# FFT filter with two feed-forward layers on one core: the second layer's weights become float32 beside the single blocks and wait in DRAM, and the sums of weights move behind a group's first products

## The chip, the cores and the metric

One core of a Trainium2 chip runs the whole program. The metric is the device time of one execution in microseconds (us); the median of three runs of the kernel before is 1181.71 us (1181.01 to 1183.72).

## The reference

```python
X = np.fft.rfft(x, axis=1)                  # x: 2 x 3008 x 256
y = np.fft.irfft(X * (filt_r + 1j * filt_i), n=3008, axis=1)   # 6016 tokens of 256
h = y @ w_in                                # 256 x 2048, float64
g = np.where(h >= 1, h, np.where(h <= -1, 0, (h + 1) ** 2 / 4))
x = g @ w_out                               # 2048 x 256
h = x @ w_in2
out = (h / (1 + np.exp(-h))) @ w_out2
```

The weights of both layers arrive as float64, 8 bytes a number.

## The kernel before, in words

**Layers.** Tokens lie along the free dimension, in 12 blocks of 500 or 502. Every product is made of float32 parts that TensorE can multiply (a high part, rounded, and a low part, the remainder): three matmuls, high by high, high by low, low by high. A layer's 2048 hidden features are 16 slices of 128; a slice `f` has a weight tile of 128x512 (its part of `w_in` in the first 256 columns, of `w_out` in the last 256).

**Weights.** For slice `f` of layer `m`, `fetch_weight` (L146) loads 128x512 int64 words by two DMAs on SyncE's queue (SP), `read_weight` (L164) has ScalarE (ACT) make two passes over the words (L167, L168), and `form_weight` (L171) has VectorE (DVE) make three (L175 to L177) and GpSimd (POOL) one addition (L178). The result is a float32 tile `wa`, of which three can live at a time. For the first layer, `split_weight` makes high and low parts of it at once.

**Single blocks.** The first six blocks of the first layer go one block and one slice at a time: 96 slots of `up` (six matmuls, then ACT's `u` and square and DVE's `g`), `split_g` (ACT's `gh` L362, DVE's `gl` L364) and, five slots later, `down` (six matmuls, L376 to L378). Beside the later slots, up to number 84, runs the rest of the Fourier transform of the second half of x (ACT, DVE and POOL make its high and low parts).

**Groups.** All other work is 72 groups (`group`, L596): nine pairs of blocks (three of the first layer, called wide here, then six of the second), eight groups `j` to a pair, one for each two slices. A group makes 2x2 products by Strassen's seven: its order of PE (TensorE) work is `prod` A11, A12 (bank d, L610), S2, S3, S1, S4, A22, each of three matmuls (L526 to L528), and four `between` steps, 0 to 3, each with the twelve-part `down2` of the group before split into six matmuls. ACT copies the bank `b` after A11, S2 and S1 (`s1`, `u2`, `u4`, L535), since the next product is added on top of it; DVE makes the sums c11, c22, c21 (L612, L647, L664). Each of a group's four results has a `Chain`: in a wide group ACT's `first` (L554) and `square` (L558), DVE's `last` (L563), ACT's `high` (L571) and DVE's `low` (L574); in the second layer one Silu (L550) in place of the first three. The chain "21" of a group is finished in the next one, between its first products.

**Sums of weights.** For Strassen's products each group needs sums of its weights. `sum_first` (L436, first layer) adds high and low part on DVE (L440) and makes four sums (L423 to L426); `round_first` has ACT round them, `rest_first` has POOL subtract (L433). `sum_weight`, `round_weight` and `rest_weight` (L461 to L473) do it for the second layer from its `wa` tiles: four sums on DVE, three roundings on ACT (L430), three remainders on POOL (L433), and the `wa` tiles are then free.

**Who orders it.** The order on every engine is the order of the code. `at(t, fn, ...)` puts a function into an agenda and `due(t)` calls it: t counts slots from NB on, then, from GA = NB + 96, the `between` steps, four to a group, so that GA + 4 q + i is step i of group q. Y = GA + 96 is the first group of the second layer. An engine takes its instructions in that order and waits at the first one that isn't ready; a DMA queue does so too.

In the kernel before, the agenda fetches the second layer's weights from step Y - 38 on and converts them at Y - 34 to Y + 18 (L756 to L761), so from the sixteenth wide group on. The sums for the second layer stand at Y - 26, -18, -10, -3, 3, 9, 15, 21, the first layer's at step 2 of the group two ahead of theirs (L737).

Of the kernel before, what the change touches and what calls it, by code (L numbers as in the profile page):

```python
# [9 lines left out]
F32 = mybir.dt.float32  # L10
# [4 lines left out]
I64 = mybir.dt.int64  # L15
# [18 lines left out]
NFC = DFF // 128  # L34
# [58 lines left out]
def tile_fft_conv_moe_moe(  # L93
# [10 lines left out]
):  # L104
    nc = tc.nc
    ctx.enter_context(tc.manual_schedule())
    HEAD, LAG = 17, 5
    SP, P0, P1, P2, P3, NBX, SZ = 27, 5, 3, 2, 2, 8, 7
    WARM = 6
    CR, CF, CS, CP, RATE, TAIL = 3, 4, 7, 12, 16, 3  # L110
# [3 lines left out]
    dram = ctx.enter_context(tc.tile_pool(name="dram", bufs=1, space=bass.MemoryType.DRAM))  # L114
    W0 = 6
    wp0 = ctx.enter_context(tc.tile_pool(name="wp0", bufs=W0))
    rawp = ctx.enter_context(tc.tile_pool(name="rawp", bufs=2))
# [8 lines left out]

    x2d = dram.tile([2, 128, NTOK], F32, name="x2d")

    nc.scalar.dma_start(fwd1, dft[:96, :128])
    fwd2 = dft_sb[:, 0:128]  # L130
    inv2 = dft_sb[:, 128:256]
# [4 lines left out]
    weights, cv = {}, {}  # L136

    raws = [0]

    def raw_tile(shape, dtype, name, one=False):  # L140

        raws[0] = 0 if one else raws[0] + 1
        tag, bufs = ("raw", 1) if one or raws[0] % 3 == 1 else ("raw2", 2)
        return rawp.tile(shape, dtype, tag=tag, name=name, bufs=bufs)

    def fetch_weight(m, f):  # L146
        w_in, w_out = ((w_in1, w_out1), (w_in2, w_out2))[m]
        raw = raw_tile([128, 512], I64, f"raw{m}_{f}", m == 1 and f < 8)
        nc.sync.dma_start(
            raw[:, :256].rearrange("p (k j) -> p k j", k=2),  # L150
            w_in[:, f * 128:(f + 1) * 128].rearrange("(k p) j -> p k j", p=128),
        )
        nc.sync.dma_start(raw[:, 256:], w_out[f * 128:(f + 1) * 128, :])
        cv[m, f] = raw
# [16 lines left out]
    def form_weight(m, f):  # L171
        raw, a = cv[m, f]
        e = rawp.tile([128, 512], I32, tag="we", name=f"we{m}_{f}", bufs=1)
        ai = a.bitcast(I32)
        nc.vector.tensor_scalar(e, words(raw, I32, 1), -0x80000000, None, ALU.bitwise_and)  # L175
        nc.vector.tensor_scalar(a, a, EXP_MIN, EXP_MAX, ALU.max, ALU.min)
        nc.vector.scalar_tensor_tensor(ai, ai, 3, e, ALU.logical_shift_left, ALU.bitwise_or)  # L177
        nc.gpsimd.tensor_tensor(ai, ai, words(raw, I32, 0), ALU.add)  # L178
        cv[m, f] = a

    def split_weight(m, f, pool):
        a = cv.pop((m, f))
# [227 lines left out]
    NP = NFC // 2  # L410
# [185 lines left out]
    def group(p, j, prev, between):  # L596


        m = PL[p][0]
        wide = m == 0  # L600
# [16 lines left out]
            if not pwide:  # L617
                prev["21"].high()
        k11 = Chain(c11, p, j, "11")
        k11.first()  # L620
        if prev and not pwide:
            prev["21"].low()
        between[0]()
# [4 lines left out]
        u2 = snap(b, p, j, "u2")  # L628
        if pwide:
            prev["21"].square()  # L630
        k11.square()
        if pwide:
            prev["21"].last()
# [49 lines left out]
    NB = NCH + NBX  # L683
# [3 lines left out]
    def at(t, fn, *args):  # L687
        agenda.setdefault(t, []).append((fn, args))
# [32 lines left out]
    for i in range(HEAD, n):  # L721
        t = B1 + SP * (i - HEAD) // 10
# [10 lines left out]
    GA = NB + W1S  # L733
    Y = GA + 4 * NP * (len(PAIRS) - NS // 2)
    for j in range(NP):
        at(GA - 6 + 4 * j, sum_first, j)
        at(GA - 5 + 4 * j, round_first, j)  # L737
        at(GA - 4 + 4 * j, rest_first, j)
    zw = []

    def store(j):
# [11 lines left out]
        s = small_store(f"1_{j}") if j < 6 else [v[:, :384] for v in full[j]]  # L753
        return a, b, s

    for j, t in enumerate((-26, -18, -10, -3, 3, 9, 15, 21)):  # L756
        for i in range(2):
            f = 2 * j + i
            at(Y + t - (9 if j > 3 else 12) + (2 if j > 3 else 4) * i, fetch_weight, 1, f)
            at(Y + t - (6 if j > 3 else 8) + (2 if j > 3 else 4) * i, read_weight, 1, f)  # L760
            at(Y + t - (5 if j > 3 else 7) + (2 if j > 3 else 4) * i, form_weight, 1, f)  # L761
        at(Y + t, sum_weight, j)
        at(Y + t + 1, round_weight, j, store)
        at(Y + t + 2, rest_weight, j)

    def make_ring():
        xr = zp.tile([128, 8, 2, 512], F32R, tag="z0", name="xr")
# [144 lines left out]
```

## Time and profile before

| what | value |
|---|---|
| median of three runs | 1181.71 us |
| the profiled execution: its own time, its span | 1183.22 us, 1181.4 us |
| PE busy | 1133.7 us, 96% of the span, 4931 matmuls |
| ACT, DVE, POOL busy | 817.8, 776.1, 252.1 us |
| mean granted TensorE clock | 0.993 |
| DMA | 55.29 MB, 47 GB/s over the span |

PE is the engine that is busy throughout. Matmuls overlap in the profile, each shown with about 0.39 us while one starts every 0.23 us, so a busy PE may still start fewer matmuls than it could; the starts of the same product in successive groups show the pace better. A wait that belongs to PE or its weight load (PEld) is time lost; a wait of another engine is lost only where PE waits behind it. The clock is 2.4 GHz where it is granted as 1.0, and 1.2 GHz at 0.5.

### The profile page before, as it was taken

Reading aid. Unit: us, or ns where it says so; the run is one execution under the profiler, and the core shown is the slowest. Engines: PE = TensorE matmul, PEld = TensorE weight load, DVE = VectorE, ACT = ScalarE, POOL = GpSimd, SP = SyncE. Lnnn points to the kernel's source line nnn. Section 1 sums busy time; section 2 is a strip of 40 time slices with the busy share of each in tenths; the row PEclk is TensorE's granted clock in tenths of the full one; section 3 lists DMA queues with packets and bytes.
Section 4 is the critical chain, followed back from the end, with each engine's and each line's share of the span. In section 5 each row is a group of like instructions: output and inputs, shape, how many; then the busy total and the mean of one; then the engine's idle time right before and its main releaser. Section 6 shows DMA issues by size and latency. Waiting matters only on the chain. (4 is left out here: it accounts for less than half of the span.)

```text
span 1181.4 us, 14064 instructions
## 1 busy us (share of the span) xinstructions
PE 1133.7 (96%) x4931; PEld 901.7 (76%) x4931; DVE 776.1 (66%) x1226; ACT 817.8 (69%) x1515; POOL 252.1 (21%) x220
## 2 busy tenths in 40 slices
PE   8899999999999999999888889999999999999998
PEld 3477787878888867877666567888888888888887
DVE  6977546666657787677888878545545555555443
ACT  3588767767757777788777776766666666666664
POOL 4677534546401110000132333100000000000000
PEclk9999999999999999999999999999999999999999
DMA  9733022222000000100311140020010200200000
GB/s 241 196 97 101 1 82 61 78 56 82 15 18 1 18 1 1 54 1 1 108 51 36 56 157 1 1 70 1 26 45 1 71 1 1 70 1 1 36 1 36
DMA packets 30983, 55.29 MB, mean 47 GB/s; under 512 B 3552, under 2 KB 18112, under 8 KB 30912
## 3 DMA queue, kind: packets, MB, share of 16 engines
q1 hardware_dynamic: 27200, 47.98, 13.7%
q10 hardware_dynamic: 3712, 6.40, 1.5%
q8 instruction: 39, 0.64, 0.2%
q14 instruction: 32, 0.26, 0.1%
HBM read 42.05 MB, written 12.32 MB: 46 GB/s over the span
## 5 line engine op out<-in xcount | busy, mean ns | idle before, releaser
L377 PE MATMUL o<-gl,wh 128*128 128x502 f32 (+1 forms) x624 | 246.1, 394 | 6.3 <-DVE gl L574 6.2
L376 PE MATMUL o<-gh,wh 128*128 128x502 f32 (+1 forms) x624 | 245.9, 394 | 0.4 <-ACT ob L384 0.3
L378 PE MATMUL o<-gh,wl 128*128 128x502 f32 (+1 forms) x624 | 245.2, 393 | 0.0
L574 DVE TENSOR_TENSOR gl<-c,gh 128x502 fp32r<-128x502 f32 (+1 forms) x288 | 203.4, 720 | 55.2 <-ACT gh L571 53.4
L571 ACT ACTIVATE gh<-c 128x502 fp32r<-128x502 f32 (+1 forms) x288 | 170.5, 618 | 18.1 <-DVE c L563 15.3
L377 PEld LDWEIGHTS o<-gl,wh 128*128 128x128 f32 x624 | 118.4, 190 | 34.4 <-DVE gl L574 10.5
L535 ACT ACTIVATE u<-b 128x502 f32<-128x502 f32 (+1 forms) x144 | 83.1, 577 | 82.6 <-PE b L528 82.6
L376 PEld LDWEIGHTS o<-gh,wh 128*128 128x128 f32 x624 | 118.5, 190 | 27.0 <-ACT ob L384 1.0
L378 PEld LDWEIGHTS o<-gh,wl 128*128 128x128 f32 x624 | 118.5, 190 | 24.6
L364 DVE TENSOR_TENSOR gl<-g,gh 128x502 fp32r<-128x502 f32 (+1 forms) x80 | 63.7, 796 | 76.5 <-ACT gh L362 76.5
L647 DVE TENSOR_TENSOR c<-c,u 128x502 f32<-128x502 f32 (+1 forms) x72 | 48.8, 678 | 94.3 <-ACT u L535 94.3
L550 ACT ACTIVATE c<-c 128x502 f32<-128x502 f32 (+1 forms) x144 | 88.7, 616 | 26.6 <-DVE c L647 25.4
L178 POOL TENSOR_TENSOR wa<-wa,raw 128x512 int32<-128x512 int32 x32 | 47.7, 1492 | 249.9 <-DVE wa L177 166.8
L362 ACT ACTIVATE gh<-g 128x502 fp32r<-128x502 f32 (+1 forms) x96 | 59.9, 623 | 58.6 <-PE o L378 42.0
L664 DVE TENSOR_TENSOR c<-c,u 128x502 f32<-128x502 f32 (+1 forms) x72 | 48.9, 679 | 61.6 <-PE c L528 61.5
L535 ACT ACTIVATE s<-b 128x502 f32<-128x502 f32 (+1 forms) x72 | 42.2, 587 | 59.4 <-PE b L528 58.5
L343 PE MATMUL h<-xh,wh 128*128 128x502 f32 (+1 forms) x192 | 76.5, 399 | 3.8 <-DVE g L356 3.8
L356 DVE SCALAR_TENSOR_TENSOR g<-u,h 128x502 f32<-128x502 f32 (+1 forms) x96 | 64.3, 670 | 23.7 <-ACT u L355 23.7
L345 PE MATMUL h<-xh,wl 128*128 128x502 f32 (+1 forms) x192 | 75.1, 391 | 1.3 <-POOL wl L187 1.3
L344 PE MATMUL h<-xl,wh 128*128 128x502 f32 (+1 forms) x192 | 74.8, 389 | 0.0
L349 ACT ACTIVATE u<-h 128x502 f32<-128x502 f32 (+1 forms) x96 | 55.5, 578 | 21.2 <-PE h L345 20.6
L612 DVE TENSOR_TENSOR c<-d,s 128x502 f32<-128x502 f32 (+1 forms) x72 | 48.9, 680 | 31.4 <-PE d L528 21.1
(197 smaller groups left out, 2409.8 us busy)
## 6 DMA issues: line engine op xcount, KB each, us to landing
f<-in_filt_dram SPq DMA_DIRECT2D x64, 192.0 KB, 4.9
raw<-in_moe_w_in_dram SPq DMA_DIRECT2D x32, 256.0 KB, 2.7
raw<-in_moe_w_out_dram SPq DMA_DIRECT2D x32, 256.0 KB, 3.0
xs<-x2d SPq DMA_DIRECT2D x8, 502.0 KB, 5.3
Z<-in_x_dram SPq DMA_DIRECT2D x16, 192.0 KB, 6.1
x<-in_x_dram SPq DMA_DIRECT2D x16, 192.0 KB, 3.1
xs<-x2d SPq DMA_DIRECT2D x4, 500.0 KB, 4.2
x2d<-ob ACTq DMA_DIRECT2D x4, 251.0 KB, 2.1
```

Of the source, the lines that this page charges most:

```text
L343: nc.tensor.matmul(h, wh[:, s], xh[:, k, :t], start=(k == 0), stop=False)
L344: nc.tensor.matmul(h, wh[:, s], xl[:, k, :t], start=False, stop=False)
L345: nc.tensor.matmul(h, wl[:, s], xh[:, k, :t], start=False, stop=(k == 1))
L356: nc.vector.scalar_tensor_tensor(g, u, 1.0, h, ALU.min, ALU.max)
L364: engine.tensor_tensor(gl, g, gh.bitcast(F32), ALU.subtract)
L376: nc.tensor.matmul(o[e], wh[:, s], gh, start=first, stop=False)
L377: nc.tensor.matmul(o[e], wh[:, s], gl, start=False, stop=False)
L378: nc.tensor.matmul(o[e], wl[:, s], gh, start=False, stop=last)
L535: nc.scalar.activation(v, src, AF.Copy)
L550: nc.scalar.activation(self.g, self.h, AF.Silu)
L571: nc.scalar.activation(self.gh, self.g, AF.Copy)
L574: nc.vector.tensor_tensor(self.gl, self.g, self.gh.bitcast(F32), ALU.subtract)
```

## The change

The conversions of the second layer move from the wide groups to the single blocks: twelve are fetched at every fourth slot from 34 to 78, four more at every second from 83 to 89, and each is converted three slots later. Each result is stored two slots after that into a DRAM tile (`put_weight`, one DMA of 256 KB on SP) and read back (`get_weight`, one DMA on SP, into one of the three `wa` buffers) for `sum_weight`, which now stands at step 0 of a group, with its roundings at step 1 and its remainders at step 2: Y - 24, -20, -16, -8, -4, 0, 4, 8. `sum_first` moves from step 2 two groups ahead to step 0 of the group just ahead of the one that uses it. In a wide group, the chain 11's first ACT instruction moves behind the copy `u2` and the square of the chain 21.

```diff
--- before.py
+++ after.py
@@ -104,7 +104,7 @@
 ):
     nc = tc.nc
     ctx.enter_context(tc.manual_schedule())
-    HEAD, LAG = 17, 5
+    HEAD, LAG, EARLY = 17, 5, 12
     SP, P0, P1, P2, P3, NBX, SZ = 27, 5, 3, 2, 2, 8, 7
     WARM = 6
     CR, CF, CS, CP, RATE, TAIL = 3, 4, 7, 12, 16, 3
@@ -126,6 +126,8 @@
 
     x2d = dram.tile([2, 128, NTOK], F32, name="x2d")
 
+    w2d = [dram.tile([128, 512], F32, name=f"w2d{f}") for f in range(NFC)]
+
     nc.scalar.dma_start(fwd1, dft[:96, :128])
     fwd2 = dft_sb[:, 0:128]
     inv2 = dft_sb[:, 128:256]
@@ -137,15 +139,17 @@
 
     raws = [0]
 
-    def raw_tile(shape, dtype, name, one=False):
-
-        raws[0] = 0 if one else raws[0] + 1
-        tag, bufs = ("raw", 1) if one or raws[0] % 3 == 1 else ("raw2", 2)
+    def raw_tile(shape, dtype, name):
+        raws[0] += 1
+        tag, bufs = ("raw", 1) if raws[0] % 3 == 1 else ("raw2", 2)
         return rawp.tile(shape, dtype, tag=tag, name=name, bufs=bufs)
 
     def fetch_weight(m, f):
         w_in, w_out = ((w_in1, w_out1), (w_in2, w_out2))[m]
-        raw = raw_tile([128, 512], I64, f"raw{m}_{f}", m == 1 and f < 8)
+        if m == 1 and f < EARLY:
+            raw = dp.tile([128, 512], I64, tag="raw", name=f"raw{m}_{f}", bufs=1)
+        else:
+            raw = raw_tile([128, 512], I64, f"raw{m}_{f}")
         nc.sync.dma_start(
             raw[:, :256].rearrange("p (k j) -> p k j", k=2),
             w_in[:, f * 128:(f + 1) * 128].rearrange("(k p) j -> p k j", p=128),
@@ -177,6 +181,13 @@
         nc.vector.scalar_tensor_tensor(ai, ai, 3, e, ALU.logical_shift_left, ALU.bitwise_or)
         nc.gpsimd.tensor_tensor(ai, ai, words(raw, I32, 0), ALU.add)
         cv[m, f] = a
+
+    def put_weight(f):
+        nc.sync.dma_start(w2d[f], cv.pop((1, f)))
+
+    def get_weight(f):
+        cv[1, f] = rawp.tile([128, 512], F32, tag="wa", name=f"wb{f}", bufs=3)
+        nc.sync.dma_start(cv[1, f], w2d[f])
 
     def split_weight(m, f, pool):
         a = cv.pop((m, f))
@@ -617,7 +628,8 @@
             if not pwide:
                 prev["21"].high()
         k11 = Chain(c11, p, j, "11")
-        k11.first()
+        if not wide:
+            k11.first()
         if prev and not pwide:
             prev["21"].low()
         between[0]()
@@ -628,6 +640,8 @@
         u2 = snap(b, p, j, "u2")
         if pwide:
             prev["21"].square()
+        if wide:
+            k11.first()
         k11.square()
         if pwide:
             prev["21"].last()
@@ -733,9 +747,9 @@
     GA = NB + W1S
     Y = GA + 4 * NP * (len(PAIRS) - NS // 2)
     for j in range(NP):
-        at(GA - 6 + 4 * j, sum_first, j)
-        at(GA - 5 + 4 * j, round_first, j)
-        at(GA - 4 + 4 * j, rest_first, j)
+        at(GA - 4 + 4 * j, sum_first, j)
+        at(GA - 3 + 4 * j, round_first, j)
+        at(GA - 2 + 4 * j, rest_first, j)
     zw = []
 
     def store(j):
@@ -753,15 +767,19 @@
         s = small_store(f"1_{j}") if j < 6 else [v[:, :384] for v in full[j]]
         return a, b, s
 
-    for j, t in enumerate((-26, -18, -10, -3, 3, 9, 15, 21)):
+    for f in range(NFC):
+        t = NB + (34 + 4 * f if f < EARLY else 83 + 2 * (f - EARLY))
+        at(t, fetch_weight, 1, f)
+        at(t + 3, read_weight, 1, f)
+        at(t + 3, form_weight, 1, f)
+        at(t + 5, put_weight, f)
+    for j in range(NP):
+        t = Y - 24 + 4 * j + (4 if j > 2 else 0)
         for i in range(2):
-            f = 2 * j + i
-            at(Y + t - (9 if j > 3 else 12) + (2 if j > 3 else 4) * i, fetch_weight, 1, f)
-            at(Y + t - (6 if j > 3 else 8) + (2 if j > 3 else 4) * i, read_weight, 1, f)
-            at(Y + t - (5 if j > 3 else 7) + (2 if j > 3 else 4) * i, form_weight, 1, f)
-        at(Y + t, sum_weight, j)
-        at(Y + t + 1, round_weight, j, store)
-        at(Y + t + 2, rest_weight, j)
+            at(t - 2 + i, get_weight, 2 * j + i)
+        at(t, sum_weight, j)
+        at(t + 1, round_weight, j, store)
+        at(t + 2, rest_weight, j)
 
     def make_ring():
         xr = zp.tile([128, 8, 2, 512], F32R, tag="z0", name="xr")
```

PE's order does not change. On ACT, in a slot of the single blocks (`u2_9` is the ninth slice of block 2, `hl` a part of the Fourier transform), before:

```order
L349 ACTIVATE u2_9_1735<-h2_9_1727 128x502
L362 ACTIVATE gh2_8_1737<-g2_8_1686 128x502
L355 ACTIVATE u2_9_1735<-u2_9_1735 128x502
L234 ACTIVATE hl18_1757<-t1_18_1725 128x384
L234 ACTIVATE hl19_1764<-x19_1651 96x512
L349 ACTIVATE u2_10_1777<-h2_10_1769 128x502
```

and in the change, whose lines are numbered 11 to 14 higher:

```order
L360 ACTIVATE u2_9_1766<-h2_9_1758 128x502
L373 ACTIVATE gh2_8_1768<-g2_8_1717 128x502
L366 ACTIVATE u2_9_1766<-u2_9_1766 128x502
L245 ACTIVATE hl18_1788<-t1_18_1756 128x384
L245 ACTIVATE hl19_1795<-x19_1678 96x512
L171 ACTIVATE wa1_1_1800<-raw1_1_1680 128x512
L172 ACTIVATE raw1_1_1680<-raw1_1_1680 128x512
L360 ACTIVATE u2_10_1816<-h2_10_1808 128x502
```

Two ACT instructions of a conversion now stand ahead of the next slot's `u`.

On ACT, in the fourth group of the third wide pair (names are chain, pair and group: `v112_3` is chain 11 of pair 2, group 3), before:

```order
L554 ACTIVATE v212_2_5688<-c212_2_5652 128x500
L554 ACTIVATE v112_3_5690<-c112_3_5685 128x500
L517 ACTIVATE xr_3228<-xs3_0_5438 128x502
L535 ACTIVATE u22_3_5702<-b2_3_5668 128x500
L558 ACTIVATE v212_2_5688<-v212_2_5688 128x500
L558 ACTIVATE v112_3_5690<-v112_3_5690 128x500
L571 ACTIVATE gh21_2_2_5708<-c212_2_5652 128x500
L535 ACTIVATE u42_3_5725<-b2_3_5668 128x500
L571 ACTIVATE gh11_2_3_5727<-c112_3_5685 128x500
L167 ACTIVATE wa1_4_5745<-raw1_4_5637 128x512
L168 ACTIVATE raw1_4_5637<-raw1_4_5637 128x512
```

and in the change:

```order
L565 ACTIVATE v212_2_5857<-c212_2_5824 128x500
L528 ACTIVATE xr_3387<-xs3_0_5621 128x502
L546 ACTIVATE u22_3_5874<-b2_3_5837 128x500
L569 ACTIVATE v212_2_5857<-v212_2_5857 128x500
L565 ACTIVATE v112_3_5877<-c112_3_5854 128x500
L569 ACTIVATE v112_3_5877<-v112_3_5877 128x500
L582 ACTIVATE gh21_2_2_5882<-c212_2_5824 128x500
L441 ACTIVATE wz_5779<-wb2_5810 128x512
L441 ACTIVATE wz_5779<-wb3_5835 128x512
L441 ACTIVATE sh1_1_5891<-ws1_1_5865 128x384
L546 ACTIVATE u42_3_5904<-b2_3_5837 128x500
```

The conversion is gone, `u2` (`u22_3`) comes ahead of `v112_3`, and three roundings of weights now stand ahead of the copy `u4` (`u42_3`).

On DVE, the sums for the first layer's sixth pair of slices (`wr5`, `ws0_5`), before, between the sums c22 and c21 of group 3:

```order
L647 TENSOR_TENSOR c220_3_4032<-c0_3_4019,u40_3_4026 128x502
L574 TENSOR_TENSOR gl11_0_3_4029<-c110_3_3984,gh11_0_3_4028 128x502
L440 TENSOR_TENSOR wr5_4041<-wh0_10_1009,wl0_10_1010 128x256
L440 TENSOR_TENSOR wr5_4041<-wh0_11_1068,wl0_11_1069 128x256
L423 TENSOR_TENSOR ws0_5_4044<-wr5_4041 128x128
...
L426 TENSOR_TENSOR ws0_5_4044<-wr5_4041,ws0_5_4044 128x128
L664 TENSOR_TENSOR c210_3_4063<-c0_3_4019,u20_3_4003 128x502
```

and in the change, in group 4:

```order
L623 TENSOR_TENSOR c110_4_4292<-d0_4_4288,s10_4_4279 128x502
L585 TENSOR_TENSOR gl12_0_3_4286<-c120_3_4265,gh12_0_3_4285 128x502
L451 TENSOR_TENSOR wr5_4303<-wh0_10_1025,wl0_10_1026 128x256
L451 TENSOR_TENSOR wr5_4303<-wh0_11_1084,wl0_11_1085 128x256
L434 TENSOR_TENSOR ws0_5_4306<-wr5_4303 128x128
...
L437 TENSOR_TENSOR ws0_5_4306<-wr5_4303,ws0_5_4306 128x128
L523 TENSOR_TENSOR xs1_0_4020<-xs1_0_4020 128x502
L574 SCALAR_TENSOR_TENSOR c210_3_4263<-v210_3_4295,c210_3_4263 128x502
```

The sums now stand behind c11 and ahead of the last step of the chain 21 (`c210_3`).

## Rows read from the trace of the kernel before

**Rows 1.** Busy time of the engines in stretches of the span: the single blocks beside the Fourier transform, the last nine wide groups, the next five groups (the second layer's first), and the 42 groups after them. Columns: from and to, length, busy us and count of PE, PEld, DVE, ACT, POOL, granted clock, DMA share, GB/s.
```profile
215.00:345.00 130.00, 127.92 (x618) 107.27 (x617) 85.12 (x126) 89.96 (x170) 56.65 (x53) 1.00 0.19 56
...
548.17:667.40 119.23, 103.34 (x406) 75.64 (x405) 98.11 (x160) 94.57 (x178) 28.44 (x19) 0.97 0.19 62
667.40:732.45 65.05, 55.98 (x226) 42.44 (x225) 51.35 (x79) 45.98 (x86) 26.08 (x19) 0.97 0.22 72
732.45:1162.52 430.07, 430.07 (x1891) 356.36 (x1890) 229.44 (x359) 280.09 (x507) 3.96 (x3) 1.00 0.06 22
```

**Rows 2.** Timeline of PE: the first matmul into bank d of groups 1, 7, 8, 9, 10, 15, 24, 29 and 71 (counted from 0). Columns: start, us, then the instruction.
```profile
383.76 0.39 PE L526 MATMUL d<-xr,wh 128*128 128x502 f32 x1
...
457.51 0.39 PE L526 MATMUL d<-xr,wh 128*128 128x502 f32 x1
...
469.63 0.39 PE L526 MATMUL d<-xr,wh 128*128 128x502 f32 x1
...
479.94 0.39 PE L526 MATMUL d<-xr,wh 128*128 128x502 f32 x1
...
495.74 0.39 PE L526 MATMUL d<-xr,wh 128*128 128x502 f32 x1
...
548.17 0.39 PE L526 MATMUL d<-xr,wh 128*128 128x502 f32 x1
...
667.40 0.38 PE L526 MATMUL d<-xr,wz 128*128 128x502 f32 x1
...
732.45 0.39 PE L526 MATMUL d<-xr,wh 128*128 128x502 f32 x1
...
1162.52 0.39 PE L526 MATMUL d<-xr,wh 128*128 128x500 f32 x1
```

**Rows 3.** Waits between 548.17 and 732.45 us: engine and line, what it waited for, us in total, times, longest.
```profile
PE b L526 <- ACT u L535: 15.1, 15, 1.8
...
ACT wa L167 <- POOL wl L433: 9.0, 4, 2.4
...
PE o L377 <- DVE gl L574: 5.4, 6, 1.5
```

**Rows 4.** Groups of instructions in the same stretch: line, engine, operation, count, busy us in total, mean ns of one, idle time before them and its releasers.
```profile
L178 POOL TENSOR_TENSOR wa<-wa,raw 128x512 int32<-128x512 int32 x16 | 23.2, 1448 | 228.1 <-DVE wa L177 164.7 <-ACT v L554 12.4 <-ACT sh L430 10.8
...
L433 POOL TENSOR_TENSOR wl<-wa,wh 128x512 fp32r<-128x512 f32 x8 | 13.3, 1678 | 0.0
L177 DVE SCALAR_TENSOR_TENSOR wa<-wa,we 128x512 int32<-128x512 int32 x16 | 11.1, 693 | 0.5
L167 ACT ACTIVATE wa<-raw 128x512 f32<-128x512 f32 x16 | 10.6, 662 | 10.1 <-POOL wl L433 9.0 <-ACT ob_9p L384 0.5 <-ACT ob_10p L384 0.5
...
L433 POOL TENSOR_TENSOR sl<-ws,sh 128x384 fp32r<-128x384 f32 x6 | 7.4, 1231 | 0.0
L175 DVE TENSOR_SCALAR we<-raw 128x512 int32<-128x512 int32 x16 | 6.9, 429 | 0.0
...
L430 ACT ACTIVATE wh<-wa 128x512 fp32r<-128x512 f32 x8 | 4.6, 618 | 0.0
```

**Rows 5.** Timeline of a wide group without conversions and without sums of weights: the last matmul of S2, ACT's and DVE's steps up to `u4` (L535 at 543.66), and the first matmul of S4.
```profile
540.39 0.39 PE L528 MATMUL b<-xr,s 128*128 128x502 f32 x1
540.59 0.67 DVE L574 TENSOR_TENSOR gl<-c,gh 128x502 fp32r<-128x502 f32 x1
...
541.29 0.57 ACT L535 ACTIVATE u<-b 128x502 f32<-128x502 f32 x1
...
542.41 1.27 DVE L563 SCALAR_TENSOR_TENSOR c<-v,c 128x502 f32<-128x502 f32 x2 [0.56 <-ACT v L558]
...
543.12 0.63 ACT L571 ACTIVATE gh<-c 128x502 fp32r<-128x502 f32 x1 [0.23 <-DVE c L563]
...
543.66 0.57 ACT L535 ACTIVATE u<-b 128x502 f32<-128x502 f32 x1
...
544.71 0.39 PE L526 MATMUL b<-xr,s 128*128 128x502 f32 x1
```

**Rows 6.** Timeline of a wide group with a conversion at step 1, ahead of `u4`.
```profile
633.35 0.65 ACT L167 ACTIVATE wa<-raw 128x512 f32<-128x512 f32 x1
...
634.45 0.57 ACT L535 ACTIVATE u<-b 128x500 f32<-128x500 f32 x1
...
635.07 0.49 PE L526 MATMUL b<-xr,sh 128*128 128x500 f32 x1 [1.15 <-ACT u L535]
```

**Rows 7.** Timeline of a wide group in which DVE and POOL both read from SBUF.
```profile
587.99 1.30 POOL L178 TENSOR_TENSOR wa<-wa,raw 128x512 int32<-128x512 int32 x1 [9.48 <-DVE wa L177]
588.13 1.69 DVE L574 TENSOR_TENSOR gl<-c,gh 128x500 fp32r<-128x500 f32 x1 [0.28 <-ACT gh L571]
...
589.88 0.49 PE L377 MATMUL o<-gl,wh 128*128 128x500 f32 x1 [1.06 <-DVE gl L574]
```

**Rows 8.** Waits in the single blocks, between 215 and 345 us.
```profile
DVE gl L364 <- ACT gh L362: 42.7, 33, 4.2
```

**Rows 9.** Groups of instructions of `sum_first` between 371.33 and 469.63 us, columns as in rows 4.
```profile
L440 DVE TENSOR_TENSOR wr<-wh,wl 128x256 f32<-128x256 f32 x12 | 4.5, 418 | 0.0
...
L423 DVE TENSOR_TENSOR ws<-wr 128x128 f32<-128x128 f32 x7 | 2.0, 293 | 0.7
```

**Rows 10.** DMA issues of the whole span: line, engine, count, KB each, median us from issue to landing.
```profile
raw<-in_moe_w_out_dram SPq DMA_DIRECT2D x32, 256.0 KB, 3.0
```

## The prediction, made before the change was run

> **What bounds the kernel now.** I read the table of stretches first, then the starts of one product group by group, then the waits of the stretch that loses time, then single timelines there. From 732.45 us to the end PE is busy all the time, and its granted clock is 1.00 [rows 1]: 42 groups take 1162.52 - 732.45 = 430.07 us [rows 2], 10.24 us each. That is PE's own pace and the yardstick for what follows; nothing after 732 us can get faster.
>
> Between 548.17 and 667.40 us nine wide groups take 119.23 us [rows 1, 2]. At 10.24 us they would take 92.2, so 27.0 us are lost. In the next five groups 65.05 - 51.2 = 13.9 us are lost. All sixteen conversions of the second layer lie in these two stretches [rows 4]. That wide groups don't need the extra time by themselves is seen in the five before them: from 495.74 to 548.17 us, without conversions and without sums of weights, they take 52.43 us [rows 2], 10.49 each. Part of the loss is the clock: 0.97 in both stretches [rows 1], so PE had about 3% of 184 us at half work, some 5 us; the rest of the span between has 1.00. The waits name who is late: PE for ACT's copies 15.1 us, PE for DVE's `gl` 5.4, and ACT's conversions for POOL's remainders 9.0, since only three `wa` tiles live [rows 3]. So the wide groups are bound by ACT and DVE, whose order has no room for more work, and the prize is at most 27.0 + 13.9 = 41 us.
>
> **What the conversions cost where they go.** One is 0.66 us twice on ACT, 0.43 twice (the second pass is of the same kind) and 0.69 on DVE, 1.45 on POOL [rows 4]. That is 1.3, 1.55 and 1.45 us, once in four slots. Between 215 and 345 us PE is busy 127.92 of 130 us, ACT only 89.96, DVE 85.12, POOL 56.65 [rows 1]. Even if all twelve of the early conversions fell into these 130 us, ACT would come to 106, DVE to 104 and POOL to 74: none reaches 130. DVE waits there 42.7 us for ACT's `gh` [rows 8], which in turn waits for PE's old `down`: these engines follow PE with a distance fixed by buffers, and a late one catches up. I charge **2 us** for the single blocks; the bounds are 0 (all of it in idle time) and 16 x 0.4 = 6 (each delays PE by a third of what rows 6 show). The four late ones stand where the transform has ended. The new DMAs are 32 of 256 KB; one of that size lands 3.0 us after issue [rows 10], and a stored tile has from the single blocks to the wide groups after 548 us. On SP a storing DMA waits for POOL's addition, and loads of the transform queue behind it; they are issued at least two slots before use, so I cost this at nothing; without that cover it is part of the 6 us.
>
> **What is left in the nine wide groups.** The change leaves five sets of second-layer sums there (steps Y - 24, -20, -16, -8, -4), each with four DVE sums, three roundings ahead of `u4`, and three remainders on POOL. A clean group shows the room [rows 5]: S2 ends at 540.39 + 0.39 = 540.78, `u2` starts only at 541.29, behind `first` of chain 11; `gh` of chain 21 starts at 543.12, `u4` at 543.66, and S4, which needs `u4`, at 544.71. ACT starts an instruction every 0.5 to 0.55 us. In the change `u2` can start at 540.8, and then square, `first`, square and `gh` follow, the last at about 542.9. But DVE has the four sums (4 x 0.3 = 1.2 us, [rows 9]) behind `gl`, which ends near 541.2, so chain 21's `last` runs from 542.5 to 543.1 and `gh` from 543.15. Three roundings of 0.52 us come next, so `u4` ends near 545.9 and S4 waits 1.2 us. The nearest row agrees: a conversion's two instructions at the same place took 1.10 us and PE waited 1.15 [rows 6]. Five times 1.2 is 6.0. In two of the five groups a sum of x (0.67 us, like any two-operand DVE step of that size) stands in the same step, 1.3 more. The first and the last of the nine make four parts of x, as group 7 did, which took 469.63 - 457.51 = 12.12 us [rows 2], 1.9 above pace; 3.0 for both with the earlier `u2`. POOL's remainders beside DVE I put at 0.3 a set, 1.5, and the remaining groups at 0.7. The sum is 12.5, so **14.5 us are gained** (27.0 - 12.5). The bounds are 21 (sets at no more than 0.2) and 7 (2.5 a set and one clock drop of 1.7).
>
> **The five groups after them.** Second-layer groups have one ACT step where wide ones have three, and 42 of them ran at PE's pace [rows 2]; a rounding between `u2` and `u4` fits there. What stopped them was ACT standing at a conversion for POOL's remainder [rows 3]; that wait moves to SP, whose DMA into the third `wa` buffer waits for the remainder instead. I leave 1.5 us for the first, which finishes wide chains, and 0.5 for the others: **11.9 us gained**, bounds 13.5 and 9.
>
> **The first layer's sums.** Their DVE work, 2 x 0.42 + 4 x 0.29 = 2.0 us [rows 9], was between c22 and c21; now it stands ahead of chain 21's `last`, and two roundings ahead of `u4`. By the timeline of rows 5 `last` then starts near 543.3 in place of 542.4, `gh` ends at 544.5, the roundings (0.53 and 0.3) at 545.3 and `u4` at 545.9: PE waits 1.2 us, or 1.9 in the three groups with a sum of x in the same step. Over groups 1 to 6 that is 3 x 1.2 + 3 x 1.9 = 9.3. Before, these six took 457.51 - 383.76 = 73.75 us [rows 2]; minus 61.4 at pace and 5.6 for loading a pair (group 9, which has that load and no sums: 495.74 - 479.94 - 10.24) the loss is 6.8. So this part **loses 2.5 us**; bounds: 3 gained (the sums fill DVE's wait of 0.56 us for the square [rows 5]) and 6 lost.
>
> **`first` of chain 11 behind `u2`.** In the wide groups with parts of x to make, outside the above, I take **0.5 us gained**, between 0 and 1.5.
>
> Sum: 14.5 + 11.9 + 0.5 - 2.5 - 2 = 22.4 us. The profiled execution took 1183.22 us, which becomes 1160.8; it is 1.5 above the median of the runs shown, 1181.71, which becomes 1159.3. I say 1160.
>
> **A row and a rule.** DVE's `gl` took 1.69 us beside a POOL addition that had begun 0.14 earlier, where it takes 0.67 alone, and PE waited 1.06 us for it [rows 5, 7]. The Trainium skill, in "SBUF — State Buffer", section "Who interferes with whom", says that a DVE instruction with two SBUF inputs and a GpSimd instruction that reads SBUF exclude each other for the whole instruction. The row agrees. By that rule the change takes sixteen exclusions out of the groups but moves them where POOL is busier, and it leaves the remainders; the third rival is what this would do.
>
> **Rivals.**
> (1) *The sums hide.* ACT and DVE catch up within the group, a set costs 0.3 us and the first layer's sums nothing extra. For it: DVE's idle 0.56 us and PE waiting 15.1 us in 15 places only [rows 3, 5]. Against: rows 6. Gain 22.4 + 5 x 0.9 + 1.3 + 4.0 (the first layer's sums gain 1.5 instead of losing 2.5) = 32.2, time 1149.
> (2) *Slower: the single blocks break.* A slot's `u` stands behind the conversion on ACT, its bank is released late, and the next `up` finds none free. The price is rows 6 and 7 together: 1.15 + 1.06 = 2.2 us for each of 16, 35 us instead of 2, so 11 slower, 1192. It decides from (22.4 + 2)/16 = 1.5 us each. Against it: 40 idle us of ACT and 45 of DVE in 130 [rows 1].
> (3) *POOL holds DVE.* Three remainders in a row (1.68, 1.68, 1.23 us, [rows 4]) each hold one two-operand DVE step by up to 1.06 [rows 7]: 5 x 3 x 1.06 = 16 instead of 1.5. Gain 8, time 1174. For it: rows 7. Against: only part of DVE's steps are waited for at once.
> (4) *The reads come late.* A tile's second half waits for POOL's remainder, then 3.0 us for landing; the next sums are due 10.2 us after the last ones, and by the durations above some 2 us are to spare. If not, DVE itself waits: 6 x 1.5 = 9 us less, 1169.
> (5) *The conversions weren't the cause*, and the wide groups lose as much without them: 1182. Against: 10.49 us a group before 548 us.
>
> **How the numbers follow.** My forecast, 1153 to 1167, has 0.52; (1) 0.20, (2) 0.05, (3) 0.15, (4) 0.06, (5) 0.02. The range of 1147 to 1174 takes in (1), (3) and (4) and leaves out the ends of these and (2) and (5). A measurement tells 0.2%, 2.4 us, from no change: faster 0.93, within it 0.02, slower 0.05.
>
> **What would show it.** Right: no conversion after 371 us; the nine groups in about 105 us, the next five in 53; PE waiting at S4 for `u4` about 1 us in groups with sums of weights; clock 1.00 in both stretches; the stretch from 215 to 345 us with PE as busy as before. Wrong: PE waits for `g` or for a bank there, DVE sums waiting for a DMA, `gl` steps of 1.5 us and more behind remainders, or the first layer's wide groups at 13 us.

## The result and the profile after

The changed kernel takes 1162.16 us (median of four runs, 1160.22 to 1163.41) against 1182.59 us (1181.01 to 1183.72) before: 20.4 us less, ratio 0.9827 with a 95% interval of 0.9805 to 0.9848. The profiled execution took 1160.99 us, 22.2 less than that of before; the sum forecast 22.4.

The table of stretches of the changed kernel, from the same group to the same group as [rows 1]:

```profile
215.00:345.00 130.00, 127.53 (x616) 106.75 (x615) 97.75 (x149) 97.91 (x185) 70.44 (x62) 1.00 0.36 115
552.88:656.33 103.45, 95.25 (x406) 76.27 (x405) 82.98 (x137) 86.88 (x163) 21.05 (x15) 0.98 0.17 51
656.33:710.26 53.93, 51.80 (x227) 42.06 (x226) 32.49 (x57) 38.98 (x72) 11.18 (x9) 1.00 0.17 58
710.26:1140.30 430.04, 430.04 (x1892) 356.34 (x1890) 227.70 (x356) 278.97 (x504) 0.00 (x0) 1.00 0.07 22
```

In the single blocks PE is as busy as before (127.53 of 130 us against 127.92) while DVE has 12.6, ACT 8.0 and POOL 13.8 us more to do. The nine wide groups take 103.45 us in place of 119.23, the next five 53.93 in place of 65.05, and the 42 after them the same 430.0.

PE's first matmul into bank d, for groups 0, 1, 7, 15, 24 and 29, as in [rows 2]:

```profile
372.73 0.79 PE L537 MATMUL d<-xr,wh 128*128 128x502 f32 x1 [2.97 <-DVE g L367]
387.22 0.39 PE L537 MATMUL d<-xr,wh 128*128 128x502 f32 x1
...
463.29 0.38 PE L537 MATMUL d<-xr,wh 128*128 128x502 f32 x1
...
552.88 0.39 PE L537 MATMUL d<-xr,wh 128*128 128x502 f32 x1
...
656.33 0.39 PE L537 MATMUL d<-xr,wz 128*128 128x502 f32 x1
...
710.26 0.39 PE L537 MATMUL d<-xr,wh 128*128 128x502 f32 x1
```

Start by start, the 22.2 us are made up so: group 1 starts 3.5 us later than before (387.22 against 383.76); groups 1 to 6 take 76.07 us in place of 73.75, 2.3 lost; groups 7 to 14 take 89.59 in place of 90.66, 1.1 gained; then 15.8 in the nine wide groups and 11.1 in the next five. The first row shows what the prediction did not have: PE waits 2.97 us for `g` at group 0, the last slice of the single blocks.

The waits between 552.88 and 710.26 us, answering to [rows 3] (us in total, times, longest):

```profile
PE b L537 <- ACT u L546: 8.3, 7, 1.6
...
PE c L537 <- DVE c L661: 2.0, 2, 1.4
...
DVE ws L434 <- DMA wb<-w2d: 1.5, 1, 1.5
```

PE's wait for ACT's copies fell from 15.1 to 8.3 us; ACT's wait for POOL's remainders at a conversion (9.0) and PE's for `gl` (5.4) are gone. The new reads were late once.

Where these 8.3 us come from shows in the timeline of group 18, which holds a set of second-layer sums (`u2` at 587.65, `u4` at 591.92, S4 in the last row):

```profile
587.65 0.59 ACT L546 ACTIVATE u<-b 128x500 f32<-128x500 f32 x1 [0.58 <-PE b L539]
588.06 0.28 DVE L434 TENSOR_TENSOR ws<-wb,wb 128x128 f32<-128x128 f32 x1
...
589.24 1.39 DVE L574 SCALAR_TENSOR_TENSOR c<-v,c 128x500 f32<-128x500 f32 x2
...
589.94 0.62 ACT L582 ACTIVATE gh<-c 128x500 fp32r<-128x500 f32 x1
590.47 1.13 ACT L441 ACTIVATE wz<-wb 128x512 fp32r<-128x512 f32 x2
...
591.51 0.51 ACT L441 ACTIVATE sh<-ws 128x384 fp32r<-128x384 f32 x1
591.92 0.56 ACT L546 ACTIVATE u<-b 128x500 f32<-128x500 f32 x1
...
592.54 0.49 PE L537 MATMUL b<-xr,sh 128*128 128x500 f32 x1 [0.87 <-ACT u L546]
```

It is the chain that the prediction drew from [rows 5]: four sums until 589.3, `last`, `gh`, three roundings, then `u4`, and PE has waited 0.87 us. In the five sets of the nine wide groups (18, 19, 20, 22 and 23) the wait is 0.87, 0.86, 1.44, 1.46 and 1.56 us; the other 2.1 us are the sets of groups 24 and 25.

How group 0 came late: the end of the single blocks, with the sums of `sum_first` for group 0 ending at 368.4, the last conversion (L179, L182), a part of x (L533) and the two steps before PE's first matmul into bank d at 372.73.

```profile
368.14 0.29 DVE L437 TENSOR_TENSOR ws<-wr,ws 128x128 f32<-128x128 f32 x1
368.35 0.42 DVE L179 TENSOR_SCALAR we<-raw 128x512 int32<-128x512 int32 x1
...
369.74 0.68 DVE L533 TENSOR_TENSOR xr<-xs,xr 128x502 fp32r<-128x502 f32 x1
370.05 1.51 POOL L182 TENSOR_TENSOR wa<-wa,raw 128x512 int32<-128x512 int32 x1 [7.32 <-DVE wa L181]
370.33 1.75 DVE L375 TENSOR_TENSOR gl<-g,gh 128x500 fp32r<-128x500 f32 x1
...
372.01 0.66 DVE L367 SCALAR_TENSOR_TENSOR g<-u,h 128x500 f32<-128x500 f32 x1
```

DVE has the sums, three passes of a conversion and a part of x in a row, and then `gl` takes 1.75 us, beside POOL's addition, where it takes 0.68 alone. And PE's clock fell; this is the stretch from 371.80 us on:

```profile
371.80:378.60 6.80, 5.87 (x14) 4.75 (x15) 5.64 (x10) 4.86 (x9) 1.56 (x2) 0.50 0.10 39
```

For these 6.8 us the granted clock was 0.50, 1.2 in place of 2.4 GHz, and group 0 took 14.49 us in place of 12.43.

Not all of the difference between the two profiles belongs to the change. The stretch from 10 to 60 us, before the moved conversions, first of before, then of the change:

```profile
10.00:60.00 50.00, 43.43 (x130) 22.95 (x131) 43.99 (x73) 23.21 (x44) 33.58 (x37) 0.93 0.85 216
```

```profile
10.00:60.00 50.00, 43.98 (x149) 22.96 (x148) 47.82 (x78) 25.93 (x49) 35.79 (x38) 1.00 0.85 216
```

The profiled execution of before had a lower clock there, and the first slot of the single blocks begins later. ACT's first `u`, first of before, then of the change:

```profile
63.69 0.56 ACT L349 ACTIVATE u<-h 128x502 f32<-128x502 f32 x1
```

```profile
61.30 0.58 ACT L360 ACTIVATE u<-h 128x502 f32<-128x502 f32 x1
```

In later kernels whose code is the change's up to there this row stands between 60.98 and 64.77 us, so these 2.4 us lie within chance. Below, the single blocks are counted from this row on.

### The profile page after: what moved, and what is told of

It reads as the page before. It is cut to its first block, busy times and chain, and to the rows that moved or that the text cites. A ratio compares the mean times of both kernels' runs of the same rounds, so it can differ in the third digit from the quotient of the medians.

```text
span 1159.2 us, 14143 instructions
## 1 busy us (share of the span) xinstructions
PE 1120.9 (97%) x4931; PEld 903.5 (78%) x4931; DVE 771.3 (67%) x1226; ACT 818.7 (71%) x1515; POOL 250.8 (22%) x220
## 4 chain that ended last, share of the span: by engine, by line
PE 77%; DVE 9%; ACT 7%; DMA 2%; issue 2%; POOL 2%; SPq 0%; DVEq 0%; ACTq 0%; POOLq 0%
PE o L387 13%; PE o L389 12%; PE o L388 12%; PE b L537 5%; PE b L538 5%; PE b L539 5%; PE h L354 3%; PE h L356 3%; PE h L355 3%; PE c L537 3%; PE xp L326 2%; PE c L538 2%; PE c L539 2%; DVE gl L585 1%; ACT gh L582 1%
## 5 line engine op out<-in xcount | busy, mean ns | idle before, releaser
L585 DVE TENSOR_TENSOR gl<-c,gh 128x502 fp32r<-128x502 f32 (+1 forms) x288 | 195.5, 693 | 61.4 <-ACT gh L582 60.9
L354 PE MATMUL h<-xh,wh 128*128 128x502 f32 (+1 forms) x192 | 76.7, 399 | 3.8 <-DVE g L367 3.8
L182 POOL TENSOR_TENSOR wa<-wa,raw 128x512 int32<-128x512 int32 x32 | 50.3, 1573 | 78.9 <-DVE wa L181 34.8
```

The source lines that it names most:

```text
L354: nc.tensor.matmul(h, wh[:, s], xh[:, k, :t], start=(k == 0), stop=False)
L585: nc.vector.tensor_tensor(self.gl, self.g, self.gh.bitcast(F32), ALU.subtract)
```

## The experiments

Times are medians of four runs beside runs of the kernel before on the same chip (1181.5, 1181.9 and 1183.3 us in the three series); ratios are to before. Groups are counted from 0; "the change" has 0.9827.

**What the conversions cost in their new place.** No conversion, store or read of the second layer's weights; its sums read other data of the same size, so the results of that layer are not those of the reference.

```diff
-    for f in range(NFC):
-        ...  # fetch, read, form, put
-        nc.sync.dma_start(cv[1, f], w2d[f])
+        nc.sync.dma_start(cv[1, f], x[0].rearrange("c p t -> (c p) t")[f * 88:f * 88 + 128, :])
```

> The change without the second layer's conversions and without their storing: the sums read float32 tiles of the same size from x instead, so the second layer's weights are wrong values. Theory (the twelve early conversions cost next to nothing, the four late ones the first group's wait of 3.0 us and the clock drop behind it): from 215 to 335 us the same to 0.5 us, group 0 about 5 us earlier done; 4 to 6 us faster than the change. Rival (the early ones cost each a few tenths): 2 us or more between 215 and 335 us.

Measured: 1156.51 us, 0.9782 (0.9767 to 0.9797). The first `u`, and the starts of groups 0 and 1:

```profile
62.80 0.58 ACT L360 ACTIVATE u<-h 128x502 f32<-128x502 f32 x1
...
370.49 0.39 PE L537 MATMUL d<-xr,wh 128*128 128x502 f32 x1
...
382.77 0.39 PE L537 MATMUL d<-xr,wh 128*128 128x502 f32 x1
```

That is 320.0 us to group 1, against 325.9 in the change (and 320.1 before): the conversions cost 5.9 us. Only 0.6 of it lies before the end of the fifth block (273.8 against 274.4 us, to the copy of its result); the rest is group 0's wait, gone here, and its clock. So the twelve beside the transform are nearly free, and the four late ones cost some 5 us.

**The conversions moved, all sums as before.** The kernel before with the move and the DRAM tiles alone; sums and `first` of chain 11 at their old steps.

```diff
-        t = Y - 24 + 4 * j + (4 if j > 2 else 0)
+        t = Y + (-26, -18, -10, -3, 3, 9, 15, 21)[j]
```

> The kernel before with the conversions moved to the single blocks and stored, and nothing else: first and second layer's sums at their old steps, chain 11's first ahead of u2. Theory (the conversions made the loss in the wide groups): nine wide groups within 4 us of the change's 103.5, groups 1 to 6 as in the kernel before, 73.8; total 1157 to 1163. Rival (the second layer's sums at step 0 and the new order of first are what makes it fit): wide groups at 110 us or more, total above 1168.

Measured: 1166.89 us, 0.9866 (0.9849 to 0.9882). Groups 1 to 6 take 73.6 us as before, the nine wide groups 106.1, groups 24 to 28 54.5. The groups go by the theory; the total is 3.9 us above the expected range, and its first `u` stands 3.2 us later than in the change's profile. So the move of the conversions alone brings some 15 of the 20 us; the moved sums and `first` are worth the rest, which is a small net of a loss and gains. At group 0 PE waits in this kernel too:

```profile
376.73 0.79 PE L537 MATMUL d<-xr,wh 128*128 128x502 f32 x1 [2.60 <-DVE g L367]
...
383.71 0.47 PE L537 MATMUL b<-xr,sh 128*128 128x502 f32 x1 [1.98 <-POOL wl L444]
```

The first layer's sums are at their old steps here, and the wait for `g` is still 2.60 us; so it does not need these sums beside the last conversion. With them at their old steps a second wait follows in the group, for POOL's remainder.

**The first layer's sums back at their old steps.**

```diff
-        at(GA - 4 + 4 * j, sum_first, j)
+        at(GA - 6 + 4 * j, sum_first, j)   # and round_first, rest_first likewise
```

> The change, with the first layer's sums, roundings and remainders back at their old steps (two groups ahead, steps 2, 3 and 0). Theory (this part of the change costs time: ahead of chain 21's last and ahead of u4): groups 1 to 6 take 73.5 us instead of 76.1; 2 to 3 us faster from these, and up to 3 more if the first group's wait goes with it. Rival (with u2 ahead of chain 11 the old steps cost as much): within 0.7 us in groups 1 to 6.

Measured: 1158.35 us, 0.9805 (0.9786 to 0.9824). Groups 1 to 6 take 70.6 us, against 76.1 in the change and 73.75 before. PE's waits in these six groups, first in the change, then here:

```profile
PE b L537 <- ACT u L546: 6.7, 6, 1.4
```

```profile
PE o L388 <- DVE gl L585: 0.8, 3, 0.3
PE c L537 <- DVE c L661: 0.6, 1, 0.6
```

So the move of these sums costs 5.5 us in these groups. Ahead of them it gives 1.4 us back: counted from the first `u`, group 1 starts after 327.3 us here and after 325.9 in the change, since PE waits 0.92 us in the last slots, 2.62 for `g` at group 0 and 1.97 for POOL's remainder in it, where the change has 2.97 alone. In all the move costs some 4 us, as the medians say (3.8). That the change lost only 2.3 against before is because its other part, `first` behind `u2`, gains some 3 in the same groups: with both at their old places the run above has 73.6. A comparison with before alone shows neither.

**The second layer's roundings behind `u4`.** One step later, and the remainders too.

```diff
-        at(t + 1, round_weight, j, store)
-        at(t + 2, rest_weight, j)
+        at(t + 2, round_weight, j, store)
+        at(t + 3, rest_weight, j)
```

> The change, with the second layer's roundings one step later (step 2, behind the copy u4) and the remainders at step 3. Theory (PE waits at S4 for u4, which stands behind three roundings): the wait of about 1.2 us in five wide groups and the first narrow one goes; the nine wide groups fall from 103.5 to 98 us, the whole by 5 to 6 us, to about 1156. Rival A (the four sums on DVE ahead of chain 21's last set the time, and the roundings only move the wait to the next step): within 1 us of the change. Rival B (the wa buffers come free 2.6 us later, so the read of the next tile is late): DVE waits for the DMA, 2 to 4 us slower than the change.

Measured: 1157.97 us, 0.9799 (0.9781 to 0.9818). In group 18, `u4` and S4 are on time (the same two rows as above, the timeline of this kernel), and in group 20 PE still waits:

```profile
590.65 0.57 ACT L546 ACTIVATE u<-b 128x500 f32<-128x500 f32 x1
...
591.69 0.39 PE L537 MATMUL b<-xr,sh 128*128 128x500 f32 x1
...
614.23 0.49 PE L537 MATMUL b<-xr,sh 128*128 128x500 f32 x1 [0.77 <-ACT u L546]
615.46 0.50 PE L537 MATMUL c<-xr,wh 128*128 128x500 f32 x1 [0.29 <-DVE c L661]
```

Groups 18, 22 and 23 take 10.15, 10.58 and 12.45 us in place of 11.33, 11.92 and 14.92, the last without a fall of the clock. Groups 19 and 20 stay at 11.24 and 11.98; by the order on ACT the roundings now delay its next steps, and that lateness would reach the next set, which was not measured by itself. In the fourteen groups PE's wait for `u4` falls from 8.3 to 2.3 us, and all its waits from 10.3 to 4.7. So the roundings were most of what S4 waited for. In group 20 what is left comes from the DVE sums: `gh`, ahead of `u4` on ACT, waits 1.31 us for `last`, which stands behind the four sums and a sum of x. The gain is 4.2 us, a little under the 5 to 6 expected.

**`first` of chain 11 ahead of `u2` again.**

```diff
-        if not wide:
-            k11.first()
+        k11.first()
...
-        if wide:
-            k11.first()
```

> The change, with chain 11's first back ahead of u2. Theory (in groups with sums, DVE's sums ahead of chain 21's last set the time of gh, whichever comes first on ACT): less than 1.5 us slower in all wide groups together. Rival (u2 ahead is what makes the room for the roundings): each of the twelve wide groups with sums 0.5 us longer, 6 us slower.

Measured: 1163.54 us, 0.9855 (0.9835 to 0.9876). Groups with parts of x get longer: 7 from 11.45 to 12.08, 11 from 10.64 to 11.02, 15 from 11.50 to 12.09, 19 from 11.32 to 11.90. Groups 1 to 6 and the sets in 18, 20 and 22 stay the same. There sums of weights stand ahead of `last` and set the time of `u4`, and an earlier `u2` gains nothing; in groups where none stand there it does, as the run with the sums back showed in groups 1 to 6. Group 19 has such sums, but also a part of x on ACT ahead of `u2`: with `first` ahead too, `last` waits 0.48 us for the square, and S4's wait grows from 0.86 to 1.41. Group 23 waits longer as well (2.02 for 1.56 us), but without a fall of the clock, and takes 13.16 us in place of 14.92; so this total owes something to the clock.

**POOL's remainders twice.** 24 more subtractions.

```diff
         for v, (h, l) in zip(cv.pop((1, j, 0)), W[1, j]):
             remainder(v, h, l)
+            remainder(v, h, l)
```

> The change, with each of the second layer's remainders made twice on POOL, 24 more in all, the same values again. Theory (POOL holds a DVE step now and then, but mostly one that nobody waits for, 0.3 us a set): 1 to 3 us slower. Rival (each remainder holds a DVE step that PE waits for, up to 1 us): 10 us and more slower; also slower by some us if the doubled remainders make the reads of the next tiles late, which DVE's wait for the DMA would show.

Measured: 1169.70 us, 0.9897 (0.9882 to 0.9912), 7.5 us slower than the change, between the two expectations. S4's wait grows in four of the eight sets: in group 19 from 0.86 to 1.60 us, in 20 from 1.44 to 2.24, in 23 from 1.56 to 2.25 and in 25 from 0.63 to 2.39. Groups 20 and 25:

```profile
617.88 0.50 PE L538 MATMUL b<-xr,sh 128*128 128x500 f32 x1 [2.24 <-ACT u L547]
...
682.40 0.79 PE L538 MATMUL b<-xr,sh 128*128 128x502 f32 x1 [2.39 <-ACT u L547]
```

In group 25 the 2.39 us come with a fall of the clock, and it takes 14.42 us in place of 11.16. So POOL can hold the chain. What the change's own remainders cost was not measured, since no run leaves them out; what its trace shows of them stands below, at the nine wide groups and the third rival.

**The four late conversions earlier.** Every third slot from 34, so that all are done by slot 82.

```diff
-        t = NB + (34 + 4 * f if f < EARLY else 83 + 2 * (f - EARLY))
+        t = NB + 34 + 3 * f          # EARLY = 16
```

> The change, with all sixteen conversions every third slot from 34 (the last is done by slot 84) instead of twelve every fourth and four at slots 86 to 92. Theory (the last conversions stand beside sum_first in the last slots, DVE comes late, PE waits 3.0 us for DVE's g at the first group's bank d, and the clock halves behind it for 6.8 us): group 0 starts at about 370 us instead of 372.7 and takes 12.4 instead of 14.5; 4 to 6 us faster, about 1156.5. Rival (the transform's slots have no room for a conversion every third slot): PE waits in the single blocks between 215 and 350 us, 2 us faster or less.

Measured: 1163.60 us, 0.9852 (0.9835 to 0.9868). Group 0's wait is gone (12.28 us), but it starts 314.9 us after the first `u`, 3.4 us later than in the change (311.4), as the rival had it: PE waits 3.7 us for `g` between 215 and 300 us, where the change has 1.3.

**All sixteen at every fourth slot from 20**, with the first layer's sums at their old steps.

```diff
+        t = NB + 20 + 4 * f          # EARLY = 16
```

> The change, with all conversions at every fourth slot from 20 on (the last done by slot 84) and the first layer's sums at their old steps. Theory (no conversion beside sum_first in the last slots, so group 0 starts on time; the old steps are 5 us cheaper): PE's 3 us wait at group 0's bank d goes, group 0 takes 12.4 us, groups 1 to 6 70.6; 1152 to 1155. Rival (what makes DVE late at group 0 is sum_first and the parts of x): the wait stays, 1157 or more.

Measured: 1162.58 us, 0.984 (0.9816 to 0.9863). Groups 0 and 1 to 6 as expected (12.42 and 70.9 us), but group 0 starts 8.9 us later than in the change, counted from the first `u`. Between 110 and 160 us PE waits 2.6 us for the first layer's low parts, which POOL makes beside these conversions, where the change has 1.3:

```profile
PE h L356 <- POOL wl L198: 2.6, 2, 1.4
```

And the timeline after that shows a second place: L326 is PE's first step of the parts of x for the next block, L179 a conversion on DVE, and `h` (L354) the next slot. First the change, then this kernel:

```profile
231.56 2.79 PE L326 MATMUL xp<-dft_sb,Z 128*128 128x60 f32 x24
...
237.80 0.50 PE L354 MATMUL h<-xh,wh 128*128 128x502 f32 x1 [1.32 <-DVE g L367]
...
243.61 0.99 DVE L179 TENSOR_SCALAR we<-raw 128x512 int32<-128x512 int32 x1
```

```profile
235.99 2.79 PE L326 MATMUL xp<-dft_sb,Z 128*128 128x60 f32 x24
...
237.08 0.82 DVE L179 TENSOR_SCALAR we<-raw 128x512 int32<-128x512 int32 x1
...
242.93 0.50 PE L354 MATMUL h<-xh,wh 128*128 128x502 f32 x1 [2.02 <-DVE g L367]
```

At the preparation of a block PE waits 1.32 us for `g` in any case. In the change the conversion comes 12 us after it starts; here, and with every third slot, 1.1 us after it (237.72 against 236.64 us in that run), and the wait is 2.02 and 2.01 us. So it matters in which slots a conversion lies. These two places are only a part: ahead of group 0 all of PE's waits add up to 14.5 us here and to 6.4 in the change (without the 2.97 at group 0), most of them for `g` and for POOL's parts. What the falls of the clock that follow add was not measured by itself.

**The two moves undone, and the late four in the phase of the others.** Two kernels: the roundings a step later and the first layer's sums back; and the same with three conversions ahead of the transform and one at slot 82.

```diff
+        t = NB + 22 + 4 * f          # EARLY = 15, the second kernel alone
```

> The change with two edits together: the second layer's roundings and remainders one step later (behind u4), and the first layer's sums back at their old steps. The conversions stay as in the change. Alone the two brought 4.2 and 3.8 us against the change's 1162.2. Theory: they act in different groups (15 to 23, and 1 to 6) and add: groups 1 to 6 in about 70.6 us, the nine wide groups in about 98.7, group 0 still with its wait of 3 us for g, total 1154.2 (1152 to 1156). Rival: what one gives the other takes back (a clock drop in group 23 or a later set that starts late): total 1157 or more, no better than either alone.

> The run before with the four late conversions moved as well: three ahead of the transform (fetched at slots 22, 26 and 30) and one at slot 82, so that all sixteen stand at every fourth slot in the phase of the change's twelve. Theory (the late four cost group 0 its wait and its clock, and a conversion in this phase costs next to nothing): group 0 starts near 371 us and takes 12.3 in place of 15, total about 1150 (1148 to 1152). Rival (any conversion outside slots 34 to 78 stands in the way, as in the run with sixteen from slot 20, where PE waited for the first layer's low parts at 130 to 136 us and for g at 230 to 290): group 0 in 12.3 but its start at 375 or later, total 1154 or more.

Measured: 1156.68 us, 0.9775 (0.9758 to 0.9793), and 1148.15 us (1145.94 to 1152.84), 0.9709 (0.9683 to 0.9734). In both, groups 1 to 6 take 70.6 us or less and the nine wide groups 98.6 or 98.7, as each edit gave alone. The first kernel's total is 2.5 us above the expected sum and outside its range; its first `u` stands at 62.86 us, 1.6 later than in the change's profile, so part of it may be chance. The second has groups 0 and 1 at:

```profile
373.02 0.39 PE L537 MATMUL d<-xr,wh 128*128 128x502 f32 x1
...
385.42 0.39 PE L537 MATMUL d<-xr,wh 128*128 128x502 f32 x1
```

Group 0 has no wait for `g` and takes 12.4 us. Counted from the first `u`, group 1 starts after 320.7 us, against 327.5 in the first kernel and 320.1 before the change. From the first `u` to the end of the fifth block it needs 274.4 us, as the change does: three more conversions in this phase cost nothing. It is 35 us faster than before and 14 faster than the change.

## Why the prediction was right, point by point

The time was right within 2.2 us between the medians, and the sum within 0.2 us between the profiles. The 0.2 is luck: the single blocks cost 3.9 us more than forecast, and 2.4 us of chance ahead of them and 1.3 us in the other terms made up for it.

| term | forecast | measured |
|---|---|---|
| nine wide groups (15 to 23) | +14.5 | +15.8 |
| groups 24 to 28 | +11.9 | +11.1 |
| `first` of 11 behind `u2`, elsewhere | +0.5 | +1.1 |
| first layer's sums, groups 1 to 6 | -2.5 | -2.3 |
| single blocks, to the start of group 1 | -2 | -5.9, and +2.4 by chance ahead of them |

*Nine wide groups.* Right, with its mechanism. Five sets at 1.2 us and two sums of x were to cost 7.3; PE's waits at S4 add up to 6.2, shorter where no sum of x stands ahead (0.87 and 0.86) and with 1.44 to 1.56 where one or more parts of x do. These are idle times; from start to start groups 18, 19, 20 and 22 are 1.1, 1.1, 1.7 and 1.7 us over the pace of 10.24. One fall of the clock (651.7 to 655.1 us, granted 0.50), which the prediction did not have, is left in group 23, behind waits of 1.56 and 1.35 us. The second of these shows POOL:

```profile
649.80 1.76 DVE L585 TENSOR_TENSOR gl<-c,gh 128x500 fp32r<-128x500 f32 x1
651.48 0.66 DVE L661 TENSOR_TENSOR c<-c,u 128x500 f32<-128x500 f32 x1
...
652.20 0.79 PE L537 MATMUL c<-xr,wh 128*128 128x500 f32 x1 [1.35 <-DVE c L661]
```

Two remainders run on POOL from 648.01 to 651.02 us and a third behind them; `gl` takes 1.76 in place of 0.68 us beside them, c22 stands behind `gl`, and PE waits for c22. So by these rows some 1.1 of the 1.35 us are the remainders'.

*Groups 24 to 28.* Right: 53.93 us, 53 forecast. The wait that moved to SP did once come back: DVE waited 1.5 us for a read in group 25, PE 0.63 behind it. Rival (4) is there in one set of eight.

*The first layer's sums.* Right as a net, 2.3, and the place was right (six waits at S4). PE was idle 0.8 to 0.9 and 1.4 us there; from start to start these groups are 1.2 (groups 2 and 3) and 1.8 us (4 to 6) over the pace, where 1.2 and 1.9 were forecast. What the forecast did not separate is that the old steps with the new `u2` would have been faster than before: the move of these sums costs 5.5 us in these groups, of which 1.4 come back ahead of them.

*Single blocks.* This is the term that was mis-sized: 2 us forecast, 5.9 measured. Twelve conversions cost 0.6 us, near the bound for "all of it in idle time". The four late ones cost 5, which the text passed over with one sentence, that they stand where the transform has ended. By the bound taken from [rows 6], 0.4 each, they could cost 1.6; in fact DVE has there a conversion, a part of x and the slowed `gl` in a row (the sums for group 0 stand ahead of them, but with these elsewhere PE still waited 2.6 us), and behind PE's wait came 6.8 us at half clock; the kernels without a conversion there have neither. The Trainium skill's rule from "SBUF — State Buffer", section "Who interferes with whom", has a part in it: `gl`, with two inputs in SBUF, ran beside POOL's addition from 370.33 and ended 0.52 us after it, which comes near an exclusion for the whole instruction (0.68 us alone). It is a part only: 1.07 of the 2.97 us.

*The rivals.* (1) falls: the sums do not hide, neither the second layer's (0.87 to 1.56 us a set) nor the first's. (2) falls for the twelve. Its outcome, a bank that comes free too late, is what happened at the last of the sixteen, but through DVE's `g` and not through ACT's `u`; and the two runs with other slots start group 0 3.4 and 8.9 us later than the change. (3) falls in its size and is there in part. A sign that the prediction named for being wrong did show: in each of the five sets one `gl` beside remainders took longer, 1.09 to 1.76 us. Only in group 23 did PE wait behind it, 1.1 us and not 16; doubling the remainders costs 7.5 us. (5) falls: the conversions alone bring 15 us.

## What to carry to other kernels

Work that moves into idle time is judged by the slots that it lands in, not by the idle sum of the stretch: look for the steps where the engine is already late (a block's preparation, the last slots before another stage), and keep it off them. Ahead of the copy that frees a bank nothing should stand that can go behind it, and of a change with several moves each is worth undoing alone: here two of them, undone, and one placed anew gave 14 us more than the whole did.

## What the runs showed that was not expected

- One wait of PE of about 3 us at group 0 was paid twice: 2.97 us in itself, and 2.1 us by 6.8 us at a granted clock of 0.50. At 651.7 us, after waits of 1.56 and 1.35 us in one group, it was 3.4 us at 0.50, 1.7 lost. Waits of 0.9 us left the clock at 1.00.
- Beside the transform the first DVE pass of a conversion took longer, 728 ns in the mean in place of 429 [rows 4], and POOL's addition 1647 in place of 1448; of the eight first passes three ran with no POOL instruction beside them and took 0.37 to 0.42 us, the other five 0.79 to 0.99:

```profile
L182 POOL TENSOR_TENSOR wa<-wa,raw 128x512 int32<-128x512 int32 x9 | 14.8, 1647 | 16.7 <-DVE wa L181 6.0 <-ACT gh L373 4.1 <-ACT s L298 2.3
...
L179 DVE TENSOR_SCALAR we<-raw 128x512 int32<-128x512 int32 x8 | 5.8, 728 | 0.0
```

  The single blocks took 0.6 us longer with all of that.
- The stores to DRAM landed 3.4 us after issue, the reads 2.8 us, medians of sixteen each.
